# A first layer's output weights in eight pieces, one batch in plain float32, three more tiles through DRAM, and a new order of issue

## The chip, the core and the metric

The kernel runs on one core of a Trainium2 chip. The metric is the device time of one execution in microseconds. The kernel before was run three times: 576.28, 576.30 and 576.47 us, median 576.3.

## What is computed

Three blocks follow one another on 2176 tokens (4 batches of 512 tokens and 32 state rows, 8 heads of 64):

```
x, state:       scores = x @ state.T / 8; xread = softmax(scores) @ state
                scores2 = state @ x.T / 8; sread = softmax(scores2) @ x
first network:  h = tokens @ w_in            (512 -> 1024)
                solu = h * softmax(h); ln = (solu - mean) / sqrt(var + 1e-6) * g_ln
                x1 = ln @ w_out              (1024 -> 512)
second network: y = mish(x1 @ w2_in) @ w2_out   (512 -> 2048 -> 512)
```

All weights of the networks arrive as 64-bit floats, tokens and state as 32-bit floats.

## The kernel before

**Tiles and stages.** Tokens are cut into 17 tiles of 128: four a batch, and one for the state rows. Tiles are numbered here by their place in the order, as the steps number them: 0 to 11 are batches 0 to 2, 12 is the tile of the state rows, 13 to 16 are batch 3. In the first network the state and `w_in` are multiplied once per batch (`s_sw`, `s_sw0`: "folded" weights, 128 x 2 x 1024), so that a tile's hidden layer is attention weights times folded weights (`s_a0`, line 530). `s_a1` computes the softmax-weighted and normalised hidden layer of a tile, `s_turn` or `s_turn_far` turns it so that the hidden dimension lies on the partitions, and `s_d` (line 616) multiplies blocks of two tiles (the last of three) with `w_out` scaled by `g_ln`. The second network runs in three passes of 6, 6 and 5 tiles, 8 pairs of hidden slices each (`s_hp`, `s_post`, `s_act`, and `s_po` in the first pass, `s_tsum`, `s_tsplit`, `s_block` in the others); the first pass also loads, narrows and splits the weights and keeps them in DRAM, the others fetch them from there.

**Rounded and plain operands.** A float32 product is mostly made of three products of operands that were rounded (type fp32r): a high part is copied by ScalarE (`hi`), and VectorE subtracts it from the source for a low part (`lo`); the terms are high x high, high x low, low x high. With a flag of A set for a batch, attention weights (`weights_of`) and folded weights (`split_sw`) are copied once, without a low part, and `s_a0` makes one plain float32 product where there were three (lines 523 to 532). Before, A is "0000".

**Narrowing.** `narrow` (line 144) turns 64-bit floats into 32-bit ones with a multiplication of the high words, a shift or scaling of the low words, an optional cast and one or two merges (lines 149 to 166). The flags W, B and T choose VectorE or ScalarE for each weight block. The output weights `w_out` come in four blocks of 1 MB, 1024 elements a partition (`s_load_w_out`, `s_w_out`, lines 283 to 288), the input weights in eight of 0.5 MB. `s_gw` (line 290) scales `w_out` and splits it.

**Turning a tile.** `s_turn` (line 570) turns half a tile at a time with four transposes on TensorE (line 575), one copy on ScalarE (579) and one subtraction on VectorE (581). `s_turn_far` (line 583) turns 32 x 32 blocks on VectorE (586), writes the tile to DRAM in one DMA (590) and reads it back in four (595), then a copy (597) and a subtraction (599; flag P may give it to GpSimd). The flag Y chooses: before, nine tiles (4, 5, 6, 9 to 13 and 15) go through DRAM.

**The order.** Every step is a generator that issues a few instructions and yields. The string `ORDER` is a list of step numbers, two characters each; each occurrence runs that step up to its next yield (lines 1143 to 1151). So the order on each engine, and on SyncE's (SP's) DMA queue, is written out by hand, and every engine works through its own instructions in that order. Other flags choose the engine of single operations: C the copies of a plain batch, X the evacuations of `s_d` (line 621), M those of the second network (871), N and Z parts of `s_a1`, Q parts of the attention, S the evacuations of `s_po` (921), V the subtraction of `s_tsplit` (941). `s_warm` (line 236) issues products that compute nothing, to keep TensorE busy at the start; R leaves out single groups of four.

```
n = 64 * CODE.index(ORDER[i]) + CODE.index(ORDER[i + 1])
if n not in live:
    step, step_args = steps[n]
    live[n] = step(*step_args)
next(live[n], None)
```

Of the kernel before, what the change touches and what calls it, by code (L numbers as in the profile page):

```python
# [22 lines left out]
P = 128  # L23
# [19 lines left out]
    A="0000",  # L43
    B="0000011100011000010010111010",
    C="000000000000",
# [31 lines left out]
    "CKBoCKCKCOCBCRCRCDBoCBBmCOBoCDBoCBCOCOBsCLCSCDB-B-CLCOCVBsCSCOBsCACVCVCSCOB_CLCACSBsCPCWCSCSAlAlBpAnAnBsApApBpCZ"
    "CSArArCDCWBpCSB9BsBsCBCMCACWCZCZCPCSCPBsCMCQDFCWCaCWCWDFCMCaBuCWCWBvBvCQDHCQDHBuBvDHCaBvDHCCBuCaDFCaCaCTBvDFBvCT"
    "CaDHBvBvBxDFCaCaCTCcCWBxCbCECcCcCEBxCbDGCdCfCdDGCdCACECACfCfCCCdCdCdCYCgDGCYCdCCCCCYCgCdDGAtAtBtCiAvAvCgBtAxAxCE"
    "AzAzCdCUBtCgCXBwCiCiCgCgCeCXDECgCjCeCUDEBwCgCXDECgDGB1CUCjBwDJCjDEB1DJCeDEChCjCeDJCjCjCeDKCbB1CeB4CjCjCbCbCjCbCm"  # L80
    "ChB4CmCmB4CeDKCnDKCECeDKCnDJCbCnCqDJCEDKCnCqCqCbCnCnByByCrCnCnCtCnCrCFCkBzCFCtCtCFCrClBzCrDLCrCrCHDLB2CHCHDLCrCr"
    "CuDLCHBzDMDLB2CuDICrDMBzCuDICwBzCkB2CFCsDIB2DIBzBzCsBzDMChClDIChDMB0ChCkDNChDMB0ClDOCFB0DOCuCHB2CuCuDOB2DOB2B2Cu"
    "DNB3DNDOB3CuCwCwChB3CuChCpDNCxCIDNDPCICvCxDPDPCvCxDSDSCxCxCxDSDPCxDSCsDPCpCxCsCGCxCpCsDTDSCsDTCyDTCyDTDQDTDQCsCo"
    "CICsCoDQCGCoDQCGCGDQDRCIDRDRDRCIDkDkDlDlDlDVCyDRDoCICyDWCyDqDoCyCzCvDqDoDoCvCvDpCvDWDqDqDVDpCzCyDpDpCyDVCzCvCvCz"
    "CzDWC0C2C0DWC0C2C2DWC0DXC0C0C3DVC3C5C0C0DVC0DUC3C5C5C1C3C3C3DXC6C1DUC3C9C6C3C3C9C9C6C4DUC6C6C6DXC-C4DXC6DUC-DXC6"
    "DAC1C6C1C-C1DADAC4DUC-C4C-C-C4C4DaDrC1DmC-DZDBDrC8C-DaDmDmC-DaDrDrDaDBC_DvDwDZDaC4DZDBC_C7DsC1DYC4DBDZDBDBDYDZDv"
    "C1DYDBDBDvDYDvDbDBDwDbDYDvDbDwD3DwDbC7D8D8D3DeDsC_DwC_DbDeC_DxD5DxDdC_DsDxD9D9DxDxDdD4EAEAC7DsDdD4D5DeDtC8DsEBEB"
# [56 lines left out]
def narrow(nc, dst, src, n):  # L144
# [25 lines left out]
def attn_moe_kernel(ctx, tc, xT, xn, bd, stT, w_in, w_out, g_ln, w2i, w2o, out):  # L170
# [891 lines left out]
    for k in range(8):  # L1062
        plan(s_gw, k)
# [143 lines left out]
```

## Time and profile before

| what | us |
|---|---|
| median of three runs | 576.3 |
| the profiled execution's own time | 576.29 |
| its span | 574.6 |
| first load has landed, first work of ScalarE | 5.77 |
| first product of the first layer (line 530) | 41.0 |
| first output product of the first network (line 616) | 67.6 |
| first product of the second network (line 860) | 221.6 |
| TensorE busy, whole span | 558.4 (97%) |
| VectorE busy | 500.2 (87%) |
| ScalarE busy | 364.2 (63%) |
| GpSimd busy | 54.5 (9%) |

PE is TensorE's matrix products, PEld its weight loads (they overlap), DVE is VectorE, ACT ScalarE, POOL GpSimd, SP SyncE, whose queue issues the DMAs. An instruction's row names its line in the kernel, its operation, out<-in by the program's names and its shape; the time in brackets behind it is how long its engine stood idle before it and what ended that. TensorE's matrix products are pipelined and their ends are modelled, so the time of one is read from the distance between starts. A plain float32 product is recorded as two instructions, a rounded one as one.

### The profile page before, as it was taken

What the parts mean: (1) busy time and instruction counts of PE and PEld (TensorE: products, weight loads), DVE (VectorE), ACT (ScalarE), POOL (GpSimd) and SP (SyncE); (2) the same over time, 40 slices, a digit from 0 to 9 for tenths busy, and PEclk for the clock granted to TensorE, in tenths of its full rate; (3) what the DMA queues carried; (4) which work ended last, traced back from release to release, by engine and by line L of the source; (5) the groups of instructions that cost most, each with busy time, mean ns of one, the idle gap of its engine ahead of it and who ended that gap; (6) DMA issues with size and microseconds to landing.
All of it is one profiled execution on the core that took longest, in us unless ns stands there. A gap on an engine that the chain in (4) does not pass through costs nothing. (4 is left out here: it accounts for less than half of the span.)

```text
span 574.6 us, 9808 instructions
## 1 busy us (share of the span) xinstructions
PE 558.4 (97%) x3557; PEld 497.6 (87%) x3557; DVE 500.2 (87%) x949; ACT 364.2 (63%) x659; POOL 54.5 (9%) x134
## 2 busy tenths in 40 slices
PE   9977999999999999999999999999999999999997
PEld 3435787899789998888988989999999999999996
DVE  5999988896668878999999996689889998889996
ACT  5997968656458956999998774542433636433340
POOL 0102212210023000000000000000000024000024
PEclk9999999999999999999999999999999999999999
DMA  8952205123206688899988699876866779888832
GB/s 345 414 200 94 74 38 165 57 75 111 74 38 220 204 292 277 307 348 391 342 312 292 249 337 320 312 264 231 327 204 250 255 263 333 302 293 332 293 144 92
DMA packets 47279, 136.04 MB, mean 237 GB/s; under 512 B 5376, under 2 KB 20864, under 8 KB 46720
## 3 DMA queue, kind: packets, MB, share of 16 engines
q1 hardware_dynamic: 47232, 135.42, 66.3%
q8 instruction: 28, 0.46, 0.3%
q14 instruction: 19, 0.16, 0.1%
HBM read 96.60 MB, written 38.80 MB: 236 GB/s over the span
## 5 line engine op out<-in xcount | busy, mean ns | idle before, releaser
L860 PE MATMUL hp<-xo,w2r 128*128 128x384 f32 (+1 forms) x504 | 94.3, 328 | 0.1
L860 PEld LDWEIGHTS hp<-xo,w2r 128*128 128x128 f32 x504 | 84.8, 188 | 3.1 <-DVE u L874 0.4
L860 PE MATMUL hp<-xo,w2swh 128*128 128x384 f32 (+1 forms) x336 | 83.3, 331 | 2.0 <-DVE c L882 0.5
L616 PE MATMUL pm<-ln_l,gw_hi 128*128 128x256 f32 (+1 forms) x256 | 77.6, 303 | 0.6 <-ACT raw_c L621 0.5
L616 PE MATMUL pm<-ln_h,gw_hi 128*128 128x256 f32 (+1 forms) x256 | 74.9, 293 | 0.0
L616 PE MATMUL pm<-ln_h,gw_lo 128*128 128x256 f32 (+1 forms) x256 | 74.5, 291 | 0.0
L972 DVE TENSOR_TENSOR acc<-po,acc 128x384 f32<-128x384 f32 (+1 forms) x136 | 68.4, 521 | 3.6 <-PE po L967 3.1
L860 PEld LDWEIGHTS hp<-xo,w2swh 128*128 128x128 f32 x336 | 59.1, 188 | 6.2 <-DVE c L882 1.6
L901 ACT ACTIVATE gh<-c 128x384 fp32r<-128x384 f32 (+1 forms) x57 | 29.2, 519 | 53.2 <-DVE c L882 47.8
L860 PE MATMUL hp<-xo,w2swl 128*128 128x384 f32 (+1 forms) x168 | 55.0, 328 | 0.0
L616 PEld LDWEIGHTS pm<-ln_l,gw_hi 128*128 128x128 f32 x256 | 48.3, 189 | 4.5 <-DVE ln_l L581 1.1
L939 ACT CAST qh<-t 128x384 fp32r<-128x384 f32 (+1 forms) x60 | 28.4, 489 | 35.6 <-DVE t L931 18.0
L882 DVE TENSOR_TENSOR c<-hp,u 128x384 f32<-128x384 f32 (+1 forms) x72 | 38.0, 532 | 13.4 <-PE hp L860 12.9
L616 PEld LDWEIGHTS pm<-ln_h,gw_hi 128*128 128x128 f32 x256 | 48.2, 188 | 1.2 <-issue 0.7
L616 PEld LDWEIGHTS pm<-ln_h,gw_lo 128*128 128x128 f32 x256 | 48.6, 190 | 0.0
L530 PE MATMUL ph<-swh,aT 128*128 128x512 f32 x128 | 40.5, 405 | 3.8 <-ACT ph L548 2.5
L965 PE MATMUL po<-ql,w2oh 128*128 128x384 f32 (+1 forms) x120 | 39.5, 330 | 0.2 <-DVE acc L972 0.2
L966 PE MATMUL po<-qh,w2oh 128*128 128x384 f32 (+1 forms) x120 | 38.8, 324 | 0.0
L967 PE MATMUL po<-qh,w2ol 128*128 128x384 f32 (+1 forms) x120 | 38.8, 323 | 0.0
L159 ACT CAST w<-w 128x512 f16<-128x512 f32 x22 | 30.7, 1394 | 3.2 <-DVE w L156 2.8
L941 DVE TENSOR_TENSOR ql<-t,qh 128x384 fp32r<-128x384 f32 (+1 forms) x60 | 30.9, 533 | 1.1 <-ACT qh L939 0.6
L860 PEld LDWEIGHTS hp<-xo,w2swl 128*128 128x128 f32 x168 | 31.5, 188 | 0.0
(454 smaller groups left out, 1355.2 us busy)
## 6 DMA issues: line engine op xcount, KB each, us to landing
w2r<-ki SPq DMA_DIRECT2D x16, 768.0 KB, 6.1
w2ol<-ko SPq DMA_DIRECT2D x15, 768.0 KB, 6.3
w2oh<-ko SPq DMA_DIRECT2D x15, 768.0 KB, 6.0
w<-in_w2i SPq DMA_DIRECT2D x16, 512.0 KB, 5.4
w2swl<-ki SPq DMA_DIRECT2D x8, 896.0 KB, 6.7
w2swh<-ki SPq DMA_DIRECT2D x8, 896.0 KB, 7.5
w<-in_w2o SPq DMA_DIRECT2D x12, 512.0 KB, 5.5
ki<-w2r SPq DMA_DIRECT2D x8, 768.0 KB, 8.8
```

Source lines behind the costliest of these rows:

```text
L159: nc.scalar.copy(out=src.bitcast(F16)[..., 1], in_=f32(high))
L530: nc.tensor.matmul(out=ph[:, hf * 512:(hf + 1) * 512], lhsT=a_[:, c * P:(c + 1) * P], rhs=w_[:, q, hf * 512:(hf + 1) * 512], start=q == 0 ...
L616: nc.tensor.matmul(out=pm[:, :n], lhsT=w_[:, k, m * P:(m + 1) * P], rhs=l_[:, c0:c0 + 4 * len(blk), k, :], start=k == 0 and j == 0, stop=k ...
L860: nc.tensor.matmul(out=r, lhsT=w_[:, 0, k * P:(k + 1) * P], rhs=x_[:, k, :n], start=s in (0, 1, 3, 4) and cnt == 0, stop=cnt == 5, skip_gr ...
L882: nc.vector.tensor_tensor(out=c, in0=bank[ps, fp, s], in1=u, op=ALU.add)
L901: nc.scalar.activation(out=gh, in_=src, func=AF.Mish)
L939: nc.scalar.copy(out=hi, in_=src)
L941: on('V', ((ps - 1) * NFP + fp) * 4 + int(name[1]) - 1).tensor_tensor(out=lo, in0=src, in1=f32(hi), op=ALU.subtract)
L965: nc.tensor.matmul(out=r, lhsT=wh[:, a, c], rhs=x[1], start=first or not held, stop=False)
L966: nc.tensor.matmul(out=r, lhsT=wh[:, a, c], rhs=x[0], start=False, stop=False)
L967: nc.tensor.matmul(out=r, lhsT=wl[:, a, c], rhs=x[0], start=False, stop=last or not held)
L972: on.tensor_tensor(out=o, in0=x, in1=y, op=ALU.add)
```

## The change

The output weights are loaded and narrowed in eight pieces of 0.5 MB. Flag A sets batch 0 to plain float32. Y sends tiles 7, 8 and 14 through DRAM too, twelve in all. Most flags that choose engines are new, and `ORDER` is new from the first step to the last. Two branches are added that the flags leave unused (`nplain`, for which D must begin with 1, and a multiplication on GpSimd under flag I). The diff, without the order string:

```diff
 FLAGS = dict(
-    A="0000",
-    B="0000011100011000010010111010",
-    C="000000000000",
+    A="1000",
+    B="10101011000111100000000011100111",
+    C="110000001000",
+    D="00000",
...
+    I="00000000000000000000000000000000",
...
-    M="001100001110000000000010",
-    N="00010001110010001",
+    M="001000000010000001100000",
+    N="00000001101001111",
...
-    P="00000000000000000",
-    Q="111011111111110101010001",
-    R="0101011101110000",
-    S="000110",
-    T="1101111110001010111111111110",
+    P="00001000000100000",
+    Q="101111011011110101010001",
+    R="0101111101110000",
+    S="110011",
+    T="11001001100000001000111111111110",
...
-    V="0000000000000000000000000000000000000000000000000000000000000000",
-    W="1101010100000001111000000000",
-    X="00111010001100100101010001000101",
-    Y="00001110011111010",
-    Z="11101011110011101",
+    V="0000000000000000000000000001000000000000000000000000000000000000",
+    W="00100000000100100001101001000111",
+    X="01000000100000000001000000000100",
+    Y="00001111111111110",
+    Z="11110111001100100",
 )
...
 ORDER = (
...
-    if eng('W', n, False, True):
+    if eng('I', n, False, True):
+        nc.gpsimd.tensor_scalar(out=f32(high), in0=f32(high), scalar1=REBIAS, scalar2=None, op0=ALU.mult)
+    elif eng('W', n, False, True):
...
-    def s_load_w_out(j):
-        nc.sync.dma_start(out=wo_t(j), in_=w_out[j])
-        yield
-
-    def s_w_out(j):
-        yield from narrow(nc, f32(wo_t(j)[..., 0]), wo_t(j), 8 + j)
+    def s_load_w_out(k):
+        nc.sync.dma_start(out=wo_t(k // 2)[:, k % 2], in_=w_out[k])
+        yield
+
+    def s_w_out(k):
+        src = wo_t(k // 2)[:, k % 2]
+        yield from narrow(nc, f32(src[..., 0]), src, 8 + k)
+
+
+    nplain = int(FLAGS['D'][0])
...
+        if i < 2 * nplain:
+            copy_on('D', 1 + 2 * i + hf)(out=f32(lo), in_=tr)
+            return
...
+            if bi < nplain:
+                terms = ((f32(gw_lo), f32(ln_lo)),)
...
-        yield from narrow(nc, f32(room[..., 0]), room, 12 + f)
+        yield from narrow(nc, f32(room[..., 0]), room, 16 + f)
...
-    for j in range(4):
-        plan(s_load_w_out, j)
-        plan(s_w_out, j)
+    for k in range(8):
+        plan(s_load_w_out, k)
+        plan(s_w_out, k)
...
-    w_out = moe_w_out.reshape(4, 2, P, 512).transpose(0, 2, 1, 3)
+    w_out = moe_w_out.reshape(8, P, 512)
```

The new order begins with the output weights' pieces 2, 3, 6, 7 and 4, two halves of the input weights, piece 5, and the other halves and tokens; pieces 1 and 0 come last, as block 0 did before.

## Rows read from the trace of the kernel before

**Rows 1.** The page's busy times: engine, busy us (share of the span), instructions.
```profile
PE 558.4 (97%) x3557; PEld 497.6 (87%) x3557; DVE 500.2 (87%) x949; ACT 364.2 (63%) x659; POOL 54.5 (9%) x134
```

**Rows 2.** By source line: durations (ns), first and last start.
```profile
L530 PE MATMUL ph<-swh,aT x128: 387/393/503, 41.0 to 178.6; 128*128 128x512 f32 x128
...
L616 PE MATMUL pm<-ln_l,gw_hi x256: 280/283/684, 67.6 to 221.1; 128*128 128x256 f32 x112, 128*128 128x384 f32 x16
```

**Rows 3.** Windows: length, busy PE, PEld, DVE, ACT, POOL; clock, DMA share, GB/s.
```profile
5.77:41.00 35.23, 30.82 (x200) 14.36 (x198) 34.10 (x51) 33.64 (x43) 1.96 (x4) 1.00 0.86 334
41.00:67.60 26.60, 22.22 (x181) 16.31 (x181) 26.31 (x47) 22.43 (x43) 7.54 (x28) 1.00 0.35 115
...
148.00:221.60 73.60, 72.97 (x469) 66.28 (x468) 59.51 (x92) 48.52 (x76) 9.33 (x27) 1.00 0.55 183
221.60:283.00 61.40, 59.95 (x297) 52.40 (x295) 59.09 (x128) 58.69 (x98) 0.00 (x0) 1.00 0.94 338
283.00:345.00 62.00, 61.41 (x304) 54.61 (x304) 60.04 (x127) 52.39 (x100) 0.00 (x0) 1.00 0.83 300
345.00:459.60 114.60, 114.60 (x647) 112.56 (x646) 96.09 (x189) 52.04 (x109) 0.00 (x0) 1.00 0.77 271
```

**Rows 4.** Timeline of ACT: start, length, instruction, [idle before <- released by].
```profile
5.77 1.19 ACT L151 ACTIVATE wo<-wo 128x1024 f32<-128x1024 f32 x1 [3.77 <-DMA wo<-in_w_out]
8.29 1.19 ACT L151 ACTIVATE wo<-wo 128x1024 f32<-128x1024 f32 x1 [1.33 <-DMA wo<-in_w_out]
```

**Rows 5.** Lines by form: busy us, mean ns | idle before: what Part 2 counts.
```profile
L488 DVE TENSOR_TENSOR swl<-ph,swh 128x1024 fp32r<-128x1024 f32 x4 | 4.9, 1215 | 0.2 <-ACT swh L486 0.2
...
L581 DVE TENSOR_TENSOR ln_l<-tr,ln_h 128x512 fp32r<-128x512 f32 x16 | 10.8, 681 | 0.2 <-ACT ln_h L579 0.2
...
L156 DVE TENSOR_SCALAR wo<-wo 128x1024 uint32<-128x1024 uint32 x3 | 2.1, 690 | 4.8 <-DMA wo<-in_w_out 4.8
L161 DVE SCALAR_TENSOR_TENSOR wo<-wo 128x1024 uint32<-128x1024 uint32 x4 | 4.9, 1220 | 0.6 <-ACT wo L151 0.5
L165 DVE SCALAR_TENSOR_TENSOR wo<-wo 128x1024 uint32<-128x1024 uint32 x3 | 3.7, 1226 | 0.1
...
L156 DVE TENSOR_SCALAR wi<-wi 128x512 uint32<-128x512 uint32 x5 | 2.1, 436 | 0.0
L161 DVE SCALAR_TENSOR_TENSOR w_in_t<-wi 128x512 uint32<-128x512 uint32 x6 | 4.0, 694 | 0.0
L165 DVE SCALAR_TENSOR_TENSOR w_in_t<-wi 128x512 uint32<-128x512 uint32 x1 | 0.7, 685 | 0.0
```

**Rows 6.** Timeline of TensorE's weight loads for plain products (line 517).
```profile
157.00 0.19 PEld L517 LDWEIGHTS ph<-w_in_t,xs 128*128 128x128 f32 x1 [0.24 <-issue]
157.43 0.19 PEld L517 LDWEIGHTS ph<-w_in_t,xs 128*128 128x128 f32 x1 [0.24 <-issue]
```

**Rows 7.** Timeline of TensorE: four transposes, six rounded products, products of line 616.
```profile
110.84 0.60 PE L575 MATMUL tr<-ident,ez 128*128 128x128 f32 x4
111.20 0.48 PE L530 MATMUL ph<-swh,aT 128*128 128x512 f32 x1
...
160.30 0.63 PE L530 MATMUL ph<-swh,aT 128*128 128x512 f32 x2
...
161.70 0.28 PE L616 MATMUL pm<-ln_l,gw_hi 128*128 128x256 f32 x1
161.82 0.29 PE L616 MATMUL pm<-ln_h,gw_hi 128*128 128x256 f32 x1
```

**Rows 8.** Lines by form: a turn through DRAM on DVE, a subtraction on POOL.
```profile
L586 DVE STREAM_TRANSPOSE tt<-ez 128x1024 f32<-128x1024 f32 x9 | 11.1, 1236 | 0.9 <-ACT ez L559 0.9
L599 DVE TENSOR_TENSOR ln_l<-ln_l,ln_h 128x1024 fp32r<-128x1024 f32 x9 | 10.9, 1220 | 2.8 <-ACT ln_h L597 2.8
...
L972 POOL TENSOR_TENSOR acc<-acc,acc 128x384 f32<-128x384 f32 x4 | 4.7, 1186 | 2.8 <-DVE acc L972 2.8
```

**Rows 9.** Timeline of DVE: tile 4's turn and its last subtraction.
```profile
77.70 1.25 DVE L586 STREAM_TRANSPOSE tt<-ez 128x1024 f32<-128x1024 f32 x1
...
106.67 1.22 DVE L599 TENSOR_TENSOR ln_l<-ln_l,ln_h 128x1024 fp32r<-128x1024 f32 x1
```

More of the change, by code (lines that the diff above doesn't have):

```diff
@@ L77 @@
[L77 to L81, printed above, removed]
@@ L127 @@
-    "P_PqPuP_P9P-PtP9PtP-PuPvP-PuPwPvQBP4PwQBPxQCQBPyQCPxP3QCPzPzPyP2P0P0PzP9P9PzP1P0P-P-QDQAP0P1QAQEQDQDP1P2QFQEQAQE"
-    "P2QGP3QFQHQFPzP4QJQGQHQGP0QIQHQKQIQIQJQKQJQK"
+    "AAAABIBIBKBKBQBQATBSBSBMBMARARAUAUBABABJBJBJBCBCBLBLBJBLBOBOBRBRAWAWATBLBWADADBRA-A-BTBTBXAJAJBTA0A0BNBRANANAYAY"
+    "BNBTAQAQAaAaBaBNBbABABBXA8A8BBBNBcBBBbBYAOAOBBA2A2BDBYAPAPBDBBA6A6BPBfBWAVAVBPBaBcBDBPBfBfAXAXBPA_BpBpA_CBA4A4A1"
+    "A_A1CBBGBGBcBDBZBEBEBcBcA_A1BZBmASASCBA1BmBmA9CBBdAcAcA3CCBqBqA9A3BdA3AZAZBoBoAbAbCDCCBgBgA7AeAeA3CCA9A7A7AgAgBd"
@@ new lines @@
+    "A5A7BhBhA5CDAiAiA9BjBjBHA5CDBnBnAdAdA5BFCBBdAfAfBiBiCCBrCCCEBHBkBFByBHCEBdCDBHBvCCBFBdBdCEByBFBvCDByBeAhAhCEBlAj"
+    "AjBeBsBsBvBUBVCRBUBlBVAkAkBtCFAmAmBwBtAoAoCHCFCRCRAqAqCFBtCHCHBtCFCFCECHCVBtCSCEBtCSCVCVBtBtBtCSCGBwCGCWBzBzCSCS"
+    "CSBwCICWCZCSBwAsAsCJAuAuCSBwAwAwCWCSCJAyAyBuCZCZB0BuCWCWCWCLBuCLCJCaCdCWCLCWB0CaCJCLBwCGCGCTB0CWBwCdCdCaCICTBwCa"
+    "BwCICaCaCTBxAlAlCeCXAnAnBxCaChApApCXArArBxCaCeB3CYCXB0ChChCaB3CeDMCYDMCHB3CeCICUCeCeCiDKDKCUCYCeCiB2CUCeB0B3CbCi"
+    "CeDKDMCiB0CbB0CMB0CiCiDKCbDMB2B3CiCkB3CMCiB3CiB3CkCkB2DMCKClB5DKClDLCjCMB5DLClCjCgCKDLB5CgClClClCKCKDLCLCgAtAtCc"
@@ L129 @@
+    "O5PIPJPIPIPJPMPAPAQAQAPJPJPMPDPDP-PMPLO6P-P-PNPOPlPNO6PPPOO8PmPOO7PPPRPlO8POPOPlPNPSO7PmO-O9O-PlO9PRO_PmPdPdPiO_"
+    "PQPTPiPiPQPUPkPTPePePkPkPUPnPVPnPSPWPVPlPWPnPYPmPlPYPaPmPXPaPpPlPlPXPpPqPpPcPqPmPmPZPqPoQCPZPrQCPcQDPrPsPbPrQCPb"
+    "PtPuPrPrPxPtPwPsPgPgPxQEPwPfPfQEPuPzQBQBPvQDPyP_P_PvQCPzQEPzQCQDPyQCQDPyP0QDP1P0QGP6P1QGP2QHQGP7QHP2P3QHP4P4P3P8"
+    "P5P5P4QCQCP4QIP5QDQDQJQFP5P6QFQIP9QIP6P7QKQJQFQJP7QLP8QKQMP4QKP9QLQNQMP5QLQOQMQNQPQNQOQPQOQP"
 )
@@ L292, in s_gw @@
         g_k = g_t[:, k:k + 1]
+        if nplain:
+            nc.scalar.activation(out=f32(gw_lo[:, k]), in_=w, func=AF.Copy, scale=g_k)
+            yield
+            return
         nc.scalar.activation(out=gw_hi[:, k], in_=w, func=AF.Copy, scale=g_k)
@@ L296, in s_gw, with s_gw_split @@
                                        op0=ALU.mult, op1=ALU.subtract)
+    def s_gw_split(j):
+        hi, lo = (t[:, 2 * j:2 * j + 2] for t in (gw_hi, gw_lo))
+        nc.scalar.copy(out=hi, in_=f32(lo))
+        yield
+        nc.vector.tensor_tensor(out=lo, in0=f32(lo), in1=f32(hi), op=ALU.subtract)
     def of_head(j):
@@ L614, in s_d @@
         for k in range(8):
-            for j, (w_, l_) in enumerate(((gw_hi, ln_lo), (gw_hi, ln_hi), (gw_lo, ln_hi))):
+            terms = ((gw_hi, ln_lo), (gw_hi, ln_hi), (gw_lo, ln_hi))
+            if bi < nplain:
+                terms = ((f32(gw_lo), f32(ln_lo)),)
+            for j, (w_, l_) in enumerate(terms):
                 nc.tensor.matmul(out=pm[:, :n], lhsT=w_[:, k, m * P:(m + 1) * P], rhs=l_[:, c0:c0 + 4 * len(blk), k, :],
-                                 start=k == 0 and j == 0, stop=k == 7 and j == 2)
+                                 start=k == 0 and j == 0, stop=k == 7 and j == len(terms) - 1)
             if k % 2:
@@ L1058, in attn_moe_kernel @@
             plan(s_w_in, p, h)
-    for j in range(4):
-        plan(s_load_w_out, j)
-        plan(s_w_out, j)
+    for k in range(8):
+        plan(s_load_w_out, k)
+        plan(s_w_out, k)
     for k in range(8):
         plan(s_gw, k)
+    if nplain:
+        for j in range(4):
+            plan(s_gw_split, j)
     plan(s_tok_scores, 0)
```

96 lines of the change are left out of this document (46 added, 50 removed).

## The prediction

> **What bounds the kernel now.** I read the whole page first, then the stretches between the points where TensorE takes up new work, and only then single waits. Over the whole span TensorE (PE) is busy 97% [rows 1], but that share hides three regimes. Their borders are the first matmul of the first layer at 41.0 us and the first of its output product at 67.6 us [rows 2].
>
> From the first landing, 5.77 us, to 41 us the two evacuation engines are the bound: VectorE (DVE) is busy 34.10 and ScalarE (ACT) 33.64 of 35.23 us; PE's 30.82 contain warm-up matmuls that compute nothing [rows 3]. From 41 to 67.6 us DVE alone is the bound, 26.31 of 26.60 us, with ACT at 22.43 and PE at 22.22 [rows 3]. After that PE decides: 72.97 of 73.60 us before the second network, with DVE at only 59.51 [rows 3]. The second network's first pass is mixed: 59.95 PE, 59.09 DVE, 58.69 ACT of 61.40 us; the next pass is PE's again, 114.60 of 114.60, with DVE at 96.09 [rows 3]. So work taken from DVE pays before 67.6 us, work taken from PE pays from there to 221.6 us, and in the first pass each of three engines can take a gain back.
>
> All sums start from the profiled execution: span 574.6, its own time 576.29 us, so 1.7 us lie around the span; the median of the runs is 576.3, the same.
>
> **What does not happen.** The flag for a plain first output block (D) starts with 0 and all of I are 0, so `s_gw`, `s_d` and their new branches stay as they were. "First batch in plain float32" is flag A alone: attention weights and folded input weights of batch 0.
>
> **Part 1, the pieces.** ACT and DVE cannot start before the first 1 MB of output weights has landed: ACT waits 3.77 us until 5.77, and takes the next megabyte at 8.29, 2.5 us later [rows 4]. The new first load is half as large, so it should land 1.25 us earlier. Up to the last half of the input weights, both orders put the same bytes in the queue (3 MB of output weights, 4 MB of input weights, 1 MB and 0.5 MB of tokens), so the end of the loading does not move; the engines, nearly full from 5.77 on, gain a head start. Bounds: 0, if the early pieces only make them wait later, and -1.7, if DVE's saving below also lands here. I take -1.3, nearest to half of the 2.5.
> The Trainium skill (Perfetto Trace Analysis, DMA Optimizations) says that splitting a transfer helps to start sooner when the DMA engines are generally idle. Here their share is 0.86 in this stretch [rows 3], so by that condition the term would be 0 and the sum 1.3 us higher; this is the first half of the first rival below.
>
> **Part 2, DVE's work before 67.6 us.** Batch 0 no longer needs its low halves: two 1024-wide subtractions at 1.215 and two 512-wide ones at 0.681 go, -3.8 [rows 5]. Narrowing the output weights took DVE 3 x 0.690 + 4 x 1.220 + 3 x 1.226 = 10.6 us; in eight pieces, by the new flags, 6 scalar operations at 0.436, 8 x 0.694 and 7 x 0.685, together 13.0: +2.4 [rows 5]. For the input weights six scalar operations leave (10 to 4) and three second merges come (1 to 4): 6 x 0.436 against 3 x 0.685, -0.6 [rows 5]. Sum -2.0. The copies that remain of batch 0 stay on ACT (flag C) at the same sizes, so ACT has no saving; its slack of 4.2 us between 41 and 67.6 [rows 3] leaves most of DVE's gain to be had. Bounds 0 and -2.1; I take -1.5, near the full sum, because the row shows DVE without any slack.
>
> **Part 3, plain matmuls.** PE now does 4 plain products for each of the four tiles of batch 0 in place of 12 rounded ones. The nearest row is exact: line 517 has the same shape, each product is two instructions (8 products, 16 records), and weight loads follow each other by 0.43 us [rows 6], so a product is 0.86. Six rounded products take 160.30 to 161.70, 0.233 each [rows 7]. Four tiles: 4 x (4 x 0.86 - 12 x 0.233) = +2.6 us of PE. It lies wholly before 67.6 us, beside 26.60 - 22.22 = 4.4 us of idle PE [rows 3]: cost 0, and up to +2.6 if that idle time isn't where the tiles are. The removed warm-up group is idle-filling work; the granted clock is 1.00, its full 2.4 GHz level, in every stretch [rows 3], and the long first group and seven short ones remain: 0.
>
> **Part 4, three more tiles through DRAM (7, 8, 14).** Each loses two groups of four transposes, 0.36 us a group (110.84 to 111.20) [rows 7]: 3 x 2 x 0.36 = -2.1 us of PE, in PE's own regime, so I count it in full; the bound on the other side is 0, if the tiles come late. DVE exchanges 2 x 0.681 for 1.236 + 1.220 [rows 8], +1.1 a tile, and hands the subtractions of tiles 4 and 11 to GpSimd (POOL), -2.4: +0.9, covered by DVE's 14 us of slack before 221.6 [rows 3]. A 1024-wide subtraction on POOL has no row; a 384-wide one takes 1.186 [rows 8], so 1.2 to 3.2 us; I take 3.2, covered by more than ten us between these tiles' end and their product. Fifteen more DMAs enter SP's queue; behind tile 14's stand the first loads of the second network, which need not come before about 221 us.
>
> **Part 5, flags and order after that.** The second network's narrowing moves ten instructions from ACT to DVE, eight scalar and two merges: 8 x 0.436 + 2 x 0.685 = +4.9 us of DVE [rows 5] in or just ahead of the pass where DVE is at 96% [rows 3]. Against it, nine evacuations of `s_d` leave DVE earlier, and the new order issues more of the next pass's operand sums after that pass has begun, where DVE has 18 us to spare [rows 3]. I take 0; bounds -2.0 (1.45 us of PE's idle time in that stretch, and a little behind it) and +4.9.
>
> **Sum:** 576.3 - 1.3 - 1.5 - 2.1 = 571.4 us.
>
> **Rivals.**
> - *Only the transposes count.* The head start is lost because the queue is full, and ACT, at 33.64 of 35.23 us, holds what DVE saves. For it: ACT's row is nearly as full as DVE's [rows 3]. Against: DVE alone is full after 41 us. 576.3 - 2.1 = 574.2.
> - *The first pass takes it back.* DVE's extra 4.9 us are on the path: 571.4 + 4.9 = 576.3. Against: part of that work is issued before 221.6, where DVE idles.
> - *PE's sum decides throughout,* since 97% is its share: +2.6 - 2.1 = 576.8. Against: 4.4 us of idle PE exactly where the plain products go.
> - *Everything is paid out:* -1.7, -2.1, -2.1, all of the first pass's bound of 2.0 and the 0.6 us that PE idles before 221.6 [rows 3]: 567.8.
> - *Slower: tile 14 comes late.* Between the issue of its turn and its product PE has 192 matmuls at 0.12 [rows 7] and two groups of transposes, 23.8 us. Tile 4's path took 77.70 to 106.67 + 1.22, 30.2 us [rows 9]. If tile 14, whose loads share SP with two neighbours and the first big weight loads, is as slow, the last product of the first network waits 6.4 us: 577.8. It decides once the path exceeds 23.8 us. Against: tile 4's path had a blocked queue behind a busy slot, not slow transfers.
>
> **How the numbers follow.** Forecast 0.46; transposes only 0.17; everything paid out 0.05; these are faster, 0.68. The pass takes it back 0.12, PE's sum 0.05: no change, 0.17. Tile 14 late 0.15: slower. "No change" is within 0.2%, 1.15 us, about what a measurement of this kernel can tell. The range 567.5 to 577.0 reaches from the case that pays out everything to the one where PE's sum decides and leaves out tile 14's; the forecast's own range is 570 to 573.
>
> **What would show it.** Right: first ACT work near 4.5 us, first product of the first layer near 39.7, the output product's start near 64.8, and 5 us less up to the first matmul of the second network (about 216.7); transposes of line 575 down from 64 to 40. Wrong: a first layer that starts at 41 with ACT full; a wait of that last product on tile 14's subtraction; more idle PE between 221.6 and 345 with DVE near 100%. A PE that idles as much as before between 41 and 67.6 despite the longer products would mean that a chain, not DVE's load, sets that stretch.

## The result, and the profile after

The changed kernel takes **579.6 us** (median of 8 runs, 575.8 to 580.9) against 576.1 us for the kernel before, measured beside it (8 runs, 575.2 to 576.5). The ratio is 1.0055, 95% interval 1.0031 to 1.0079: slower, by little but clear of the interval, where 571.4 had been forecast, and outside the range. The profiled execution took 580.9 us, the longest of the eight; its span is 578.0, so 2.9 us lie outside the span (1.7 before).

TensorE's share of the page is the same 97% as in [rows 1], so the page's first part shows nothing of it:

```profile
PE 557.9 (97%) x3513; PEld 493.5 (85%) x3513; DVE 506.4 (88%) x956; ACT 355.6 (62%) x662; POOL 58.5 (10%) x132
```

First and last start of three lines of the changed kernel (durations in ns first): the first layer's products, the output products, which answer to [rows 2], and the second network's first products.

```profile
L548 PE MATMUL ph<-swh,aT x128: 387/396/792, 38.4 to 175.9; 128*128 128x512 f32 x128
...
L640 PE MATMUL pm<-ln_l,gw_hi x256: 279/283/447, 62.4 to 222.2; 128*128 128x256 f32 x112, 128*128 128x384 f32 x16
...
L884 PE MATMUL hp<-xo,w2swh x336: 306/336/522, 222.7 to 552.2; 128*128 128x384 f32 x112, 128*128 128x320 f32 x56
```

ACT's first work, which answers to [rows 4], starts 1.7 us earlier than before (timeline of ACT):

```profile
4.09 0.69 ACT L155 ACTIVATE wo<-wo 128x512 f32<-128x512 f32 x1 [2.09 <-DMA wo<-in_w_out]
```

The early gain came, and it was larger than forecast: the first layer starts 2.6 us earlier (38.4 for 41.0), the output product 5.2 (62.4 for 67.6). But the second network starts at 222.7, 1.1 us later than before's 221.6, so 6.3 us were lost in between, and the end of the span is 3.4 us later, so 2.3 more were lost behind that. The same stretches as in [rows 3] show where, with one that was not shown of before:

```profile
5.77:41.00 35.23, 32.60 (x203) 15.43 (x202) 34.39 (x60) 33.15 (x53) 1.25 (x3) 1.00 0.89 343
41.00:67.60 26.60, 26.37 (x203) 15.83 (x202) 26.23 (x43) 23.82 (x46) 9.66 (x35) 1.00 0.31 102
67.60:148.00 80.40, 78.11 (x692) 68.39 (x691) 62.09 (x89) 50.30 (x86) 15.61 (x44) 1.00 0.35 114
148.00:221.60 73.60, 67.86 (x426) 60.78 (x425) 61.58 (x93) 42.10 (x70) 9.77 (x23) 1.00 0.55 179
221.60:283.00 61.40, 57.10 (x281) 51.25 (x280) 55.76 (x122) 54.16 (x91) 0.00 (x0) 0.97 0.88 310
283.00:345.00 62.00, 62.00 (x311) 55.96 (x310) 59.74 (x128) 50.59 (x92) 0.00 (x0) 1.00 0.92 338
```

The same stretch of before, 67.6 to 148 us:

```profile
67.60:148.00 80.40, 80.40 (x727) 70.41 (x726) 64.31 (x97) 51.25 (x86) 15.00 (x48) 1.00 0.24 80
```

PE, which never stopped there before, now idles 2.3 us from 67.6 to 148 and 5.7 from 148 to 221.6 (0.6 before [rows 3]); from 221.6 to 283 it is 4.3 (1.45 before), and there the granted clock is 0.97 of full speed on the mean. Over these stretches neither DVE nor ACT is full. So the loss is waiting, not work. PE's longest waits between 62 and 240 us (us in total, times, longest):

```profile
PE pm L640 <- ACT raw_d L645: 4.6, 3, 2.7
PE hp L884 <- ACT m L895: 3.9, 1, 3.9
PE ph L548 <- DVE swl L506: 1.3, 1, 1.3
```

**First wait, 194 to 197 us.** PE waits for ACT to empty the accumulators of the seventh block (`s_d(6)`), and ACT waits, in its own order, for a transfer. Timeline of ACT in the changed kernel:

```profile
188.24 0.50 ACT L645 COPY raw_d<-pm 128x256 f32<-128x256 f32 x1
193.53 0.67 ACT L155 ACTIVATE w<-w 128x512 f32<-128x512 f32 x1 [4.79 <-DMA w<-in_w2i]
...
196.40 0.37 ACT L645 COPY raw_d<-pm 128x256 f32<-128x256 f32 x1
```

The transfer is the second network's first input weights. SP's queue (start, length of the issue, count) of the changed kernel at that place:

```profile
186.73 0.33 SPq L664 DMA_DIRECT2D w<-in_w2i  x1
187.71 6.06 SPq L616 DMA_DIRECT2D ln_l<-td  x8
```

and of the kernel before:

```profile
186.80 0.33 SPq L640 DMA_DIRECT2D w<-in_w2i  x1
...
191.78 1.82 SPq L595 DMA_DIRECT2D ln_l<-td  x4
```

It is issued at the same time in both, at the landing of the write of tile 15 that stands ahead of it in the queue (186.71 and 186.78). But the first of eight reads of tiles 14 and 15 now follows it within a microsecond, where four of tile 15 came 5 us later. The DMA view gives its time from issue to landing (last column), in the changed kernel:

```profile
w<-in_w2i SPq DMA_DIRECT2D x1, 512.0 KB, 6.7
```

and in the kernel before:

```profile
w<-in_w2i SPq DMA_DIRECT2D x1, 512.0 KB, 3.1
```

**Second wait, 224 to 228 us.** The first copy of the second network, m1 in `s_post`, follows its forerunner on ACT at once in the kernel before (223.69). In the changed one (timeline of ACT):

```profile
223.29 0.84 ACT L816 CAST xo<-raw_a 128x768 fp32r<-128x768 f32 x1
228.32 0.48 ACT L895 COPY m<-hp 128x384 f32<-128x384 f32 x1 [4.19 <-DMA ko<-w2s]
```

ko<-w2s is the write of weight sums to DRAM for later passes, issued at 220.97 and 7.2 us under way (6.0 before). Nothing in the program's logic ties m1 to it. They share a place in memory: the sums of pair 1 lie in one of four rotating slots of a pool of the first network, and the second network's pool is laid over these slots. By the addresses of the two built programs (bytes in each partition):

```
                       before            changed
sums of pair 1, low    108480..112576    96192..100288
first m1                96192..97728     96192..97728
```

In the changed kernel the ring of slots stands one step further, and m1 comes to lie under the last write. PE's busy time (first number behind the length) in both waits, and the clock behind the second, in windows of the changed kernel:

```profile
193.50:197.00 3.50, 0.81 (x7) 0.61 (x6) 2.15 (x5) 3.23 (x7) 0.00 (x0) 1.00 0.52 158
222.70:228.40 5.70, 2.26 (x14) 1.94 (x12) 3.02 (x5) 1.29 (x3) 0.00 (x0) 1.00 0.70 276
228.40:236.00 7.60, 7.15 (x31) 7.01 (x32) 5.96 (x15) 6.21 (x11) 0.00 (x0) 0.78 0.75 277
```

Behind 5.7 us in which PE was busy for 2.26, the granted clock falls to a mean of 0.78 (that is, partly 1.2 and partly 2.4 GHz) for the next 7.6.

### The profile page after: what moved, and what is told of

Same layout as the page of the kernel before. It is cut to its first block, busy times and chain, and to the rows that moved or that the text cites. A ratio compares the mean times of both kernels' runs of the same rounds, so it can differ in the third digit from the quotient of the medians.

```text
span 578.0 us, 9801 instructions
## 1 busy us (share of the span) xinstructions
PE 557.9 (97%) x3513; PEld 493.5 (85%) x3513; DVE 506.4 (88%) x956; ACT 355.6 (62%) x662; POOL 58.5 (10%) x132
## 4 chain that ended last, share of the span: by engine, by line
PE 68%; DVE 13%; ACT 9%; DMA 6%; issue 2%; POOL 1%; SPq 0%; ACTq 0%; POOLq 0%; DVEq 0%
PE hp L884 27%; PE pm L640 8%; PE po L989 6%; PE po L990 6%; PE po L991 6%; PE po L940 3%; PE po L941 3%; PE po L939 3%; PE ph L548 3%; DMA w<-in_w2i 2%; ACT ph L566 2%; DVE ez L562 1%; DMA ko<-w2s 1%; PE po L1057 1%; DVE ez L580 1%
## 5 line engine op out<-in xcount | busy, mean ns | idle before, releaser
L640 PE MATMUL pm<-ln_l,gw_hi 128*128 128x256 f32 (+1 forms) x256 | 76.3, 298 | 5.6 <-ACT raw_d L645 4.6
L884 PEld LDWEIGHTS hp<-xo,w2swh 128*128 128x128 f32 x336 | 60.7, 191 | 6.2 <-ACT m L895 4.2
L548 PE MATMUL ph<-swh,aT 128*128 128x512 f32 x128 | 45.1, 455 | 2.3 <-DVE swl L506 1.3
L548 PEld LDWEIGHTS ph<-swh,aT 128*128 128x128 f32 x128 | 22.4, 188 | 14.2 <-issue 5.6
```

The lines of the kernel that those rows point to most:

```text
L548: nc.tensor.matmul(out=ph[:, hf * 512:(hf + 1) * 512], lhsT=a_[:, c * P:(c + 1) * P], rhs=w_[:, q, hf * 512:(hf + 1) * 512], start=q == 0 ...
L640: nc.tensor.matmul(out=pm[:, :n], lhsT=w_[:, k, m * P:(m + 1) * P], rhs=l_[:, c0:c0 + 4 * len(blk), k, :], start=k == 0 and j == 0, stop=k ...
L884: nc.tensor.matmul(out=r, lhsT=w_[:, 0, k * P:(k + 1) * P], rhs=x_[:, k, :n], start=s in (0, 1, 3, 4) and cnt == 0, stop=cnt == 5, skip_gr ...
```

## The experiments

Three theories stood at the start. Theory 1: tile 14's way through DRAM makes the first weight load late, and the evacuations queued behind it wait. Theory 2: the collision of m1 with a write. Theory 3 came up with the first results: that the order, and not the two early parts, carries the early gain. All medians, each beside the kernel before on the same chip (576.1 to 576.4 us); the views come from one profiled execution of each kernel:

| run | edit, on which kernel | median us | ratio to before, 95% |
|---|---|---|---|
| 1 | changed; tile 14 on TensorE | 576.0 | 1.0003, 0.9989 to 1.0017 |
| 2 | changed; scaling of the late load on DVE | 580.6 | 1.0073, 1.0049 to 1.0097 |
| 3 | changed; m1 at another place | 575.6 | 0.9990, 0.9975 to 1.0005 |
| 4 | changed; 2 and 3 | 576.9 | 1.0010, 0.9992 to 1.0029 |
| 5 | changed; 1 and 3 | **572.6** | 0.9937, 0.9918 to 0.9956 |
| 6 | changed; first use of the load later | 577.4 | 1.0018, 1.0001 to 1.0035 |
| 7 | before; eight pieces alone | 578.2 | 1.0027, 1.0013 to 1.0041 |
| 8 | before; plain batch 0 alone | 579.2 | 1.0038, 1.0022 to 1.0053 |
| 9 | before; 7 and 8 | 579.4 | 1.0051, 1.0031 to 1.0071 |
| 10 | changed; whole loads | 581.1 | 1.0069, 1.0046 to 1.0092 |
| 11 | changed; no plain batch | 579.7 | 1.0057, 1.0038 to 1.0076 |
| 12 | 5; tiles 7 and 8 on TensorE too | 577.6 | 1.0021, 1.0002 to 1.0040 |
| 13 | 1; m1 clear of pair 1's sums | **573.0** | 0.9934, 0.9920 to 0.9947 |
| 14 | 13; tiles 7 and 8 on TensorE too | 574.4 | 0.9961, 0.9948 to 0.9973 |
| 15 | before; m1 put under the write | 578.1 | 1.0034, 1.0023 to 1.0045 |
| 16 | 6; m1 clear | 575.2 | 0.9978, 0.9963 to 0.9993 |
| 17 | 13; first use of the load later | 573.6 | 0.9956, 0.9943 to 0.9969 |

### Runs 1 to 4: the two waits, one by one

**Run 1.** The eight places of tile 14's far turn in the order become two `s_turn` steps: the transposes beside the sixth block, copies and subtractions ahead of the load's first use.

```diff
-    Y="00001111111111110",
+    Y="00001111111111010",
```

> Undoes one of the three far turns: tile 14 is transposed on TensorE again, two groups of four; the rest of the changed kernel stays. Theory 1 (tile 14's four reads share the DMA engines with the first in_w2i load of 0.5 MB, which takes 6.72 us and lands at 193.45; ACT waits for it in order, with the evacuations of the seventh block behind it): the load lands within 4 us of its issue, TensorE's idle time between 186 and 200 us falls from 3.7 us to under 1, and with 0.7 us of transposes back on PE the time is about 577.4, 2.2 us under the changed kernel's 579.6. Rival (the load is slow by its own position or by tile 15's transfers): the load still takes over 6 us, the idle time stays, and the time is the same or 0.7 us longer.

Measured 576.0, 3.6 us less than the changed kernel. The load took 3.4 us and landed at 187.2 (193.5 in the changed kernel); 2.9 of these 6.3 us are an earlier issue (183.8), behind an earlier write of tile 15. The second network starts at 216.8, where the prediction had put it (216.7), though no other run reaches that: in runs 5, 13 and 17, with tile 14 on TensorE too, it starts at 218.6 to 219.2. But the other wait stands as it was (PE's waits, 62 to 240 us; 0.3 is what is left of the 4.6):

```profile
PE hp L884 <- ACT m L895: 4.1, 1, 4.1
...
PE pm L640 <- ACT raw_d L645: 0.3, 1, 0.3
```

Theory 1 holds, with more than its 2.2 us.

**Run 2.** ACT's operation on the late load goes to DVE (one digit of W):

```diff
-    W="00100000000100100001101001000111",
+    W="00100000000100101001101001000111",
```

> One flag of the changed kernel: the scaling of the first in_w2i load, 512 wide, runs on DVE and not on ACT, so that ACT has nothing that waits for this load ahead of the evacuation of block 6. The load and tile 14's transfers stay as they are. Theory 1: the damage is ACT's wait of 4.79 us in program order; without it PE's idle time at 194 to 197 us (2.7 us) falls under 0.7, and the time is about 577.5, 2 us shorter, though the load lands as late as before. Rival (what comes after the load is the late part, whichever engine waits): the idle time stays within 0.5 us and the time is the same, or 0.4 us longer for DVE's extra operation.

580.6, no gain (the 1.0 us more is within the spread of these runs); PE's wait is the same:

```profile
PE pm L640 <- ACT raw_d L645: 4.7, 3, 2.7
```

The expectation fell, because the wait only changed engines. DVE now met the load first (its scaling starts at 192.01), and the merge of the first output weights stood behind it in DVE's order; ACT's next operation needed that merge, and the evacuation stood behind this one.

**Run 3.** Two tiles are claimed in the pool ahead of the rest, which moves m1 and computes nothing:

```diff
         phase2["wk"] = pool_of(ctx, "wk")
+        phase2["wk"].tile([P, 384], F32R, tag="g11h", name="gh", bufs=2)
+        phase2["wk"].tile([P, 384], F32, tag="c0", name="c0")
```

> Only places in memory change: two tiles of the second network's pool are claimed ahead of the rest, so that the first copy of a hidden block (m1) no longer lies where the sums of output weights lie whose write to DRAM lands at 228.17. Theory 2 (that write, 7.2 us, holds the copy on ACT by 4.19 us and PE by 3.9, and the clock then falls to a mean of 0.78 for some us): the copy starts at about 224, PE's idle time between 222 and 229 falls from 3.9 us to under 1.5, the granted clock stays at 1.00 in 228 to 236, and the time is about 576, 3.6 us shorter. Rival (the first pass is short of ACT and DVE anyway and takes the gain back within the pass): the copy is early, but the second pass starts within 0.5 us of 347.8 and the time is the same.

575.6, 4.1 us less. ACT's timeline shows no wait ahead of m1:

```profile
222.70 0.48 ACT L897 COPY m<-hp 128x384 f32<-128x384 f32 x1
```

and the window from 222 to 236 us a full clock, with PE at 13.39 of 14 us (10.11 at a clock of 0.88 in the changed kernel):

```profile
222.00:236.00 14.00, 13.39 (x64) 10.61 (x63) 13.44 (x30) 12.61 (x21) 0.00 (x0) 1.00 0.95 336
```

The second pass starts at 342.3 in place of 347.8 (1.3 of these 5.5 us this execution had gained before the second network), so the first pass doesn't take it back. Theory 2 holds; that two tiles without any computation are worth 4 us shows the cause to be the place.

**Run 4** joins the edits of runs 2 and 3.

> The edits of the second and third run together. Theories 1 and 2 together, adding up: 579.6 - 2.0 - 3.6 = 574.0 us, under the kernel before (576.3). Rival (the second wait depends on the first: what the first gives back only makes ACT and PE wait longer for the same write, or the other way round): no better than the better of the two alone, about 576.

576.9, 1.3 us more than run 3, as run 2's edit alone gave 1.0 more; neither difference is clear of the spread. As that edit removes no wait, this says nothing on whether the losses add up; run 5 does.

### Runs 5 and 6: both waits removed, and the order around the load

**Run 5**: the edits of runs 1 and 3.

> The edits of the first and the third run together, on the changed kernel: tile 14 turned on TensorE, and m1 at another place. If the two losses are separate (crowded load before 204 us; the write under m1 at 222 to 229), they add up: the second network starts near 216.8 and the rest takes 349.8 us as in the third run, span 569.1, time about 571, 5 us under the kernel before; that is the time that the prediction gave, with all its gains. Rival (an earlier start only meets the next late transfer): PE idles 3 us or more in the first pass and the time is 574 or more.

572.6, 0.63% under the kernel before. The two gains, 3.6 and 4.1, make 7.0 together: they add up but for 0.7 us, which is within the spread. First and last start of the second network's products:

```profile
L886 PE MATMUL hp<-xo,w2swh x336: 306/336/445, 218.6 to 544.1; 128*128 128x384 f32 x112, 128*128 128x320 f32 x56
```

The start is 1.8 us later than in run 1 (216.8) with the same instructions up to there; 1.3 of it is the wait for swl that the changed kernel has too and that run 1's execution did not have. What lets it come and go was not followed up.

**Run 6** moves one place of the order:

```diff
-s_load64(0, 0)
 s_d(6, 2)
...
 s_d(6, 2)
...
 s_keep_out(0, 1, 0)
+s_load64(0, 0)
 s_load64(0, 0)
```

> Order alone: in the changed kernel the first operation on the first in_w2i load (its scaling on ACT) is issued 28 steps later, behind the evacuation of block 6's third quarter and the narrowing of the first output weights, with its shift on DVE directly behind it. Load and transfers stay. The second run only moved the waiting from ACT to DVE, and the time stayed; theory 1 in a wider form (whichever engine meets the late load first holds the other through what it had yet to issue): now neither waits ahead of the evacuation, PE's idle time of 2.7 us at 194 to 197 falls under 1, and the time is about 577.5 or less. Rival (evacuations are late because the work between is too much for ACT, or another transfer is late): idle time and time unchanged, about 580.

577.4, 2.2 us less, as expected: with both engines' first use of the load behind the evacuation, PE's waits for raw_d fell from 4.6 to 1.4 us, though tile 14's transfers stayed. The view alone would prove little, since the same waits take 2.6 and 1.7 us in runs 3 and 11, whose order is untouched there; and the interval of the median just meets the changed kernel's.

### Runs 7 to 11: where the early gain comes from

**Run 7**: the changed kernel's loading and narrowing in the order of before, each place of the order doubled, with the flags of a block for both of its halves:

```diff
-s_load_w_out(j)
+s_load_w_out(2 * j)
+s_load_w_out(2 * j + 1)
...
-s_w_out(j)
+s_w_out(2 * j)
+s_w_out(2 * j + 1)
```

> The kernel before with one part of the change: output weights loaded and narrowed in eight pieces, flags and order else those of before (each step on a megabyte becomes two on its halves). The prediction's term: first ACT work at about 4.5 in place of 5.8, first product of the first layer 1.3 us earlier than 41.0, output product 1.3 earlier, time 575.0. Bounds -1.7 and 0: if the early start is lost in later waits on loads, the first layer starts at 41 and the time is 576.3; the smaller operations cost about 2.4 us of DVE, which could even put it later.

**Run 8**: the flags of the plain batch in the kernel before.

```diff
-    A="0000",
+    A="1000",
...
-    C="000000000000",
+    C="110000001000",
```

> The kernel before with the other part alone: batch 0's attention weights and folded weights in one float32 piece, its tiles' products plain; loads, order and other flags of before. It takes 3.8 us of subtractions off DVE and adds about 2.6 us of PE before 67.6. By the prediction DVE is the bound there: the output product starts at 64 to 65 in place of 67.6, time 573 to 574. Rival (a chain and not DVE's load sets this stretch, or PE's longer products do): start at 67 or later, time 576 or more.

**Run 9**: both edits.

> The kernel before with pieces and plain batch 0 together, in the order of before. The prediction's sum (-1.3 and -1.5): first layer at 39.7, output product at 64.8, time 573.5. Theory 3 (the order is what turns both parts into time; in the old order each engine meets the next instruction of its list as late as before): the runs with one part alone had the first layer at 42.8 and 40.5 and the output product at 69.5 and 67.4; with both the output product starts at 66.5 or later and the time is 576 or more.

None of the three gains anything; their flags are those of before as well as their order. First and last start of the output products in run 7:

```profile
L640 PE MATMUL pm<-ln_l,gw_hi x256: 280/283/684, 69.5 to 223.0; 128*128 128x256 f32 x112, 128*128 128x384 f32 x16
```

in run 8:

```profile
L616 PE MATMUL pm<-ln_l,gw_hi x256: 280/283/684, 67.4 to 220.9; 128*128 128x256 f32 x112, 128*128 128x384 f32 x16
```

and in run 9:

```profile
L640 PE MATMUL pm<-ln_l,gw_hi x256: 279/283/684, 69.1 to 223.7; 128*128 128x256 f32 x112, 128*128 128x384 f32 x16
```

With pieces alone ACT starts at 4.0 in place of 5.8, but the first layer at 42.8 in place of 41.0, and 1.9 us are lost at 67.6. With the plain batch alone 3.8 us of DVE's subtractions bring 0.2. Busy times from the start to the first output product (PE, PEld, DVE, ACT, POOL as in [rows 3]) tell where they went; before, changed, run 7, run 8:

```profile
0.00:67.56 67.56, 57.73 (x392) 32.47 (x393) 60.54 (x98) 57.32 (x86) 10.22 (x39) 1.00 0.64 240
0.00:62.42 62.42, 58.52 (x368) 28.87 (x369) 57.13 (x97) 54.41 (x91) 9.25 (x36) 1.00 0.68 253
0.00:69.51 69.51, 58.88 (x392) 33.62 (x393) 61.20 (x108) 57.79 (x92) 10.23 (x39) 0.98 0.64 233
0.00:67.40 67.40, 59.53 (x376) 29.68 (x377) 57.57 (x94) 57.18 (x86) 10.39 (x39) 1.00 0.64 240
```

DVE idles 7.0 us there before, 5.3 in the changed kernel, 8.3 in run 7 and 9.8 in run 8. So run 7's loss is 0.7 us of DVE's work and 1.3 of its waiting: it waits four times for a piece, 5.9 us in all, where it waited once, 4.8 us, for a megabyte. In run 8 DVE works 3.0 us less and waits 2.8 more, 1.8 of it for PE and 0.8 for ACT at 36 to 39 us.

The time of the whole is 3.0 us longer in run 8 than before, though its second network starts at 221.5; the profiled execution was the shortest of the five (577.4), and where the others lose more is not shown.

**Run 10** loads whole megabytes in the new order:

```diff
-        nc.sync.dma_start(out=wo_t(k // 2)[:, k % 2], in_=w_out[k])
+        if k % 2 == 0:
+            nc.sync.dma_start(out=wo_t(k // 2), in_=w_out[k // 2])
...
-    w_out = moe_w_out.reshape(8, P, 512)
+    w_out = moe_w_out.reshape(4, 2, P, 512).transpose(0, 2, 1, 3)
```

> The changed kernel with the output weights loaded in four transfers of 1 MB, as before, each at the place of its first half; they are still narrowed in eight pieces, in the new order. If the smaller loads carry the early start: first ACT work at 5.7 in place of 4.1, first product of the first layer at 39.7 in place of 38.4, output product at 63.7 in place of 62.4. Theory 3 (the order carries it): first layer and output product within 0.7 us of the changed kernel's.

**Run 11** takes the plain batch out of the new order; each low part's subtraction is issued directly behind its copy:

```diff
-    A="1000",
+    A="0000",
```

> The changed kernel with batch 0 in high and low halves again (four subtractions more on DVE, 3.8 us; the rounded products back, 2.6 us less PE), each added step directly behind its copy in the order; all else new. If DVE's load is the bound in the new order: output product 3 to 4 us later than 62.4, at 65.5 to 66.5. If the order alone carries the gain: within 1 us of 62.4.

First and last start of the output products in run 10 (62.4 is the first in the changed kernel):

```profile
L641 PE MATMUL pm<-ln_l,gw_hi x256: 279/283/447, 63.4 to 221.3; 128*128 128x256 f32 x112, 128*128 128x384 f32 x16
```

and in run 11:

```profile
L640 PE MATMUL pm<-ln_l,gw_hi x256: 279/283/447, 66.2 to 221.4; 128*128 128x256 f32 x112, 128*128 128x384 f32 x16
```

In the new order the pieces are worth 1.0 us and the plain batch 3.8. That is the time of the four subtractions, but up to the output product DVE is busy only 2.8 us more in run 11 (59.94); the rest is DVE's waiting, in an order that was laid out without these four. Theory 3 fell in the form in which it was set down (the order alone). An estimate from both runs, 62.4 + 1.0 + 3.8 = 67.2, is about what the old kernel has, so the new order without the parts would gain next to nothing either; no run has it. Parts and order pay only together. "Order" here takes in the new engine flags: ACT is busy 54.2 to 54.7 us before the output product in the changed kernel and runs 10 and 11, and 57.2 to 57.8 before and in runs 7 to 9. Whether the sequence or ACT's lighter load lets the parts pay, no run separates.

Run 11 shows a second thing. Its output product starts 3.8 us later than the changed kernel's, and its second network starts at 222.0 against 222.7, at the same time of the whole (579.7 and 579.6). As long as the two waits stand, the early gain buys nothing: the late load lands at 192.9 there and at 193.5 in the changed kernel, and what follows starts by that.

### Runs 12 to 17: the far tiles' worth, and the place of m1

**Run 12** is run 5 with tiles 7 and 8 turned on TensorE too, as in the kernel before:

```diff
-    Y="00001111111111010",
+    Y="00001110011111010",
```

> The fifth run's kernel (572.6 us: tile 14 on TensorE, m1 moved) with tiles 7 and 8 turned on TensorE as well, so no far tile more than before. The prediction's term of 0.72 us of PE a tile: the second network starts 1.4 us later than 218.6 and the time is 574.0. Rival (PE has idle time where these transposes go, or their reads cost as much elsewhere as they save): within 0.5 us of 572.6, or below it.

577.6, 5.0 us more than run 5, which none had expected. ACT's timeline tells why:

```profile
224.17 0.48 ACT L897 COPY m<-hp 128x384 f32<-128x384 f32 x1 [3.71 <-DMA ko<-w2s]
```

The edit turned the ring of slots again, and the sums came to lie under the place to which m1 had been moved (100288 to 104384, m1 at 100800). It is an unplanned repetition of the changed kernel's second wait. The next runs therefore claim eight late buffers first, so that m1 lies on the last of the four slots (from 108480), which the sums of pair 1 do not use in these kernels:

```diff
+        for t_ in ("g11h", "g11l", "g10h", "g10l"):
+            phase2["wk"].tile([P, 384], F32R, tag=t_, name="gh", bufs=2)
```

**Runs 13 and 14**: with tile 14 alone, and with 7, 8 and 14, on TensorE.

> The fifth run's kernel with m1 12 KB per partition behind the pool's start: eight buffers needed only late in a hidden block (high and low parts of its lower half) are claimed first. m1 then shares no place with the sums of output weights of pair 1, wherever they lie. If the place alone counts: the fifth run again, 572 to 573, m1 not waiting for a write to DRAM. If new collisions of the late buffers cost as much: 574 or more.

> The twelfth run's kernel (tiles 7, 8 and 14 turned on TensorE) with m1 at the same place as in the run beside it. In the twelfth run the sums' slots had rotated under the moved m1, which waited for the same write again (224.02 to 224.17). Theory 2: without that the time falls from 577.6 by the wait of 3.4 us and what the clock loses to 574 or less; against the run beside it, it shows what tiles 7 and 8 are worth: the prediction's 1.4 us more, or nothing (rival, PE idles there anyway).

573.0 and 574.4: the two far tiles are worth 1.4 us, by the prediction's term of 0.72 a tile 1.44. The sizes agree, the place does not. The second network's products, run 13 and then run 14:

```profile
L886 PE MATMUL hp<-xo,w2swh x336: 306/336/446, 218.9 to 544.8; 128*128 128x384 f32 x112, 128*128 128x320 f32 x56
L886 PE MATMUL hp<-xo,w2swh x336: 305/336/446, 219.3 to 546.9; 128*128 128x384 f32 x112, 128*128 128x320 f32 x56
```

Only 0.4 us of the 1.4 stands where the second network starts, and as much between runs 5 and 12 (218.6 and 219.0): from 100 to 148 us PE is busy 1.3 us more with the transposes (47.37 for 46.05 in run 13), but most of that fills time in which run 13's PE waits. The rest comes behind 219 us, where run 14 has a wait of PE of 1.0 us for the output's evacuation (`ob`) that run 13 has not; its cause was not looked for.

**Run 15**: the same claim in the kernel before, where it puts m1 exactly under the write.

> The kernel before with eight late buffers claimed first in the second network's pool, which puts m1 exactly under the sums of pair 1, whose write landed at 226.13 while m1 started at 223.69. Theory 2: m1 waits for that write, PE idles 2.4 us more at 222 to 227, time 2 to 4 us longer, 578.5 to 580. Rival (this wait costs only in the changed kernel, where ACT and DVE are short for other reasons): within 0.7 us of 576.2.

578.1, 1.8 us longer than its neighbour's 576.3 and a little under the expected 2 to 4. Here m1 is at 108480, where the sums of the kernel before lie. PE's timeline has the wait that before did not have:

```profile
226.43 0.61 PE L862 MATMUL hp<-xo,w2swh 128*128 128x384 f32 x2 [2.58 <-ACT m L873]
```

The write landed at 225.84, and m1 started at 225.90. That order of events holds in the changed kernel (228.17 and 228.32) and in runs 2, 6 and 12 too (226.92 and 227.08, 224.43 and 224.58, 224.02 and 224.17).

**Runs 16 and 17**: the edit of run 6 with m1 clear, with tile 14 far and on TensorE.

> The changed kernel with all twelve far tiles, tile 14 among them, the first use of the first in_w2i load issued later (the edit of the sixth run) and m1 clear of the sums' slots (the edit of the thirteenth). If tile 14's harm is mainly the waiting in program order behind a late load, the two edits add up: 577.4 less about 4, 573.5, as good as the thirteenth run (573.0) with tile 14 still far. Rival (its transfers cost by themselves, whatever the order): 575 or more, with a broader spread of runs than the thirteenth's 1.4 us.

> The thirteenth run's kernel (tile 14 on TensorE, m1 clear, 573.0 us) with the first use of the load issued later as well. There the load lands at 189.6, before PE needs the evacuations behind it, so theory 1 expects nothing: 572.5 to 573.5. If the order of this first use matters even with an early load, it is under 572.

Run 16 gives 575.2 and not 573.5: order alone doesn't repair what tile 14's transfers do. PE still waits 1.8 us for raw_d, and the load lands at 193.3:

```profile
PE pm L640 <- ACT raw_d L645: 1.8, 3, 0.7
```

Run 17 (573.6) shows no gain, as expected. It differs from run 16 in tile 14 alone, which is worth 1.6 us there (the two intervals just overlap). In the profiled executions with tile 14 far, the load lands between 190.1 and 193.5 us (eight of them); with it on TensorE between 187.2 and 190.4 (six). Sometimes the load itself is slow (5.2 to 6.7 us in three of the eight, 3.5 to 3.8 in the rest, 3.2 to 3.4 in the six), sometimes the write of tile 15 ahead of it on SP's queue (6.4 us in run 16, 3.1 before): in each of these executions the load is issued when that write has landed.

## Why the prediction was wrong

**Part 4, tile 14: the step that failed first.** The prediction let fifteen more DMAs enter SP's queue and wrote that the first loads of the second network, behind tile 14's, "need not come before about 221 us". That asked when PE uses these weights. But ACT and DVE narrow them beside the first network's last blocks, from 188 us on, and the evacuations that PE waits for stand behind that in the same lists. The price was 3.6 us in run 1, and 1.6 (run 16 against run 17) even when the first use was put later. The rest of the part had the right size: 1.4 us for tiles 7 and 8 (run 14 against 13), and 64 transposes became 40. That the size agrees is in part luck, since only 0.4 us of it stands where PE is freed, before the second network; "in PE's own regime, so I count it in full" did not hold, as PE waits there in the new order.

**Part 5, flags and order after 221.6: the second step that failed.** It was set at 0, from counts of operations and engines. A new order also decides which buffer of a ring a tile gets, and so what later lies on top of it. That cost 4.1 us (run 3), and the trace of before could not show it. The far tiles have a part in it: in the program of run 12, with the new order and the far tiles of before, the sums lie one slot further (100288), where m1 at its place in the changed kernel would not meet them; no run has this. Without the collision, the time from the second network's start to the last DMA's issue is 349.4 to 351.0 us in runs 3, 4, 5, 13, 14, 16 and 17 and 350.6 before: 0.4 more to 1.2 less, within the bounds, and the feared extra work of DVE did not reach the path.

**Parts 1 and 2: right in direction, mis-sized, and for an incomplete reason.** Forecast -1.3 and -1.5 at 67.6 us; measured -5.2. DVE's own account of the 5.2 is 3.4 us less work before the output product (60.5 to 57.1) and 1.7 less idle time (7.0 to 5.3), as much as its first work starts earlier (4.1 for 5.8). The pieces' term holds in the new order (1.0 in run 10). DVE's term was too small: -2.0 had been counted and -1.5 taken. ACT, to which the prediction gave no saving, works 2.9 us less before the output product (57.3 to 54.4). The reason given, that a full engine passes on its savings, is not enough by run 8: in the old order DVE's work fell by 3.0 us, its waiting for PE and ACT rose by 2.8, and the stretch gave back 0.2, with ACT as busy as before (57.2). That fits the rival by which ACT holds what DVE saves, and it fits a list laid out for the old durations; the runs do not separate the two. The condition that was weighed there (the Trainium skill, Perfetto Trace Analysis, DMA Optimizations: splitting may help where the DMA engines are generally idle), read the other way round, would have given 0. In the new order the gain was 1.0 us with the DMA engines at 0.89; in the old one it was a loss of 1.9. So neither that condition nor the prediction named what decided here, whether the consumers' lists can use the early pieces.

**Part 3 is not contradicted.** With the longer plain products alone (run 8) the first layer starts 0.5 and the output product 0.2 us earlier than before, so they cost the stretch nothing on balance. In the changed kernel, though, PE is busy 21.17 of the 21.40 us from 41 to 62.4 (17.43 before), so the idle time on which the part counted is used up; whether that held back more of the gain is not shown.

**The rivals.** "Tile 14 comes late" had the right tile and the right sign, at 577.8 us, but another mechanism. Its path took 25.2 us (175.3 to 200.5), more than the 23.8 from which it was to decide, and still the last block (204.4) did not wait for it; the load beside its reads and the evacuations behind that did. "The first pass takes it back" named the right place for the second loss, and the wrong cause: ACT and DVE had time to spare while they waited (1.29 and 3.02 us busy of 5.70).

With both waits gone, runs 5 and 13 stand at 572.6 and 573.0, 0.72 us of it by the prediction's price for tile 14's transposes. That this is near the forecast's 571.4 is in part luck. In run 13 the output product starts 4.6 us earlier than before (63.0), where 2.8 had been forecast, and the second network only 2.7 earlier (218.9), where 4.9 had been. Between the two PE idles 3.4 us (0.6 before): waits for swl, a low half of folded weights (1.3), ph, the hidden layer's accumulators (0.7), and others of under 0.7 us, which neither theory touches and no run followed.

Of the signs that were named ahead, the early ones came (ACT at 4.1 us, first layer at 38.4, output product at 62.4, 40 transposes); the first product of the second network at 216.7 did not come, except in run 1, and PE idled more between 221.6 and 345, though with DVE far from full.

## What to carry to other kernels

When a step is moved or a transfer added, ask of every transfer near it not when its data is computed with but which engine first touches it, and what stands behind that instruction in the engine's list. A new order of allocation can put a new tile on a buffer that a DMA is still reading; after each reordering look for an engine that waits on the DMA of a tensor it has nothing to do with. A saving on a full engine can turn into waiting on that engine, as in run 8; look at its busy and its idle time up to the next stage, and try a part in the old order and the order without the part before crediting either.

## What was not expected of the hardware

- The same 0.5 MB load took between 3.1 and 6.7 us; it took at most 3.4 where tile 14 was on TensorE with the new order, and 3.5 or more where that tile's transfers ran too.
- Many kernels that wait for one of these transfers spread more from run to run: the changed kernel (8 runs) and run 12 (12 runs, m1 under the write) lie within 5.1 us, run 16 (12 runs, tile 14 far) within 4.2, but runs 13, 14 and 17 (5 runs each), which have neither wait, within 1.4, 1.2 and 1.1. It is no rule: run 5, which has neither, stands between with 3.4 (6 runs), and run 15, with m1 under the write, has 2.0 (7 runs); and a range grows with the number of runs.
